# A planned linear-attention and expert kernel: 500 further plans, moved priorities, new transfer costs

## The chip, the cores and the metric

The kernel runs on one core of a Trainium2 chip. The time is the device time of one execution in microseconds, and lower is better. The kernel before took 289.69 us, the median of five runs.

A core has a matrix engine (TensorE, PE in the profile, with PEld for its weight loads), a vector engine (VectorE, DVE), a scalar engine (ScalarE, ACT), a general engine (GpSimd, POOL), and a sync engine (SP) that here only issues transfers. Each works through its own instructions in order; semaphores join them. TensorE writes its results to PSUM, a small memory of eight banks; ScalarE or VectorE read them from there ("evict" them).

## What is computed

```python
def _attn_ref(q, k, v, f_logit):                 # (4, 8, 768, 48) each
    f = 1.0 / (1.0 + np.exp(-f_logit))
    state = np.zeros((B, H, D, D))
    for t in range(S):
        state = f[:, :, t, :, None] * state + np.einsum('bhd,bhe->bhde', k[:, :, t], v[:, :, t])
        y[:, :, t] = np.einsum('bhd,bhde->bhe', q[:, :, t], state)
    return y

def _moe_ref(x, domain_probs, w1, w2):           # x (3072, 384), 4 experts, F = 1024
    p = domain_probs / (domain_probs.sum(-1, keepdims=True) + 1e-09)
    for e in range(E):
        h = np.maximum(x @ w1[e], 0.0)
        out += p[:, e:e + 1] * (h @ w2[e])
    return out
```

The attention's y, put side by side over the eight heads, is the experts' x. All four experts see all rows.

## The kernel before

The sequence of 768 is cut into six chunks `c` of 128 tokens, each with four batches `b`. For a chunk and batch the attention has these steps: `gate1` and `gate2` (ScalarE, the logarithm of the gate), `cs` (TensorE, a running sum by a triangular matrix), `exps` (ScalarE), the products `q` and `k` (VectorE or GpSimd), a transpose of them (`tpq`, `tpk` on TensorE for the first six pairs of chunk and batch, later a transposing DMA `tp` from the SP queue), `at` (TensorE, the scores), `ev_at0/1` (VectorE, with the mask), `y` (TensorE), its eviction `ev_y` or `ev_x0` to `ev_x3`, and a transpose `xt` (on TensorE with an eviction `ev_xt` for the first pairs, later a DMA). `kv`, `ev_kv` and `state` carry the state to the next chunk.

For the experts, `h c.e.fc.n0` is a unit of TensorE that computes block `fc` of expert `e`'s hidden layer for chunk `c`, from token column `n0` on (L410; three matmuls of 512 columns, or six of 128 in the first units of all), and `relu` of the same number evicts it on ScalarE (L421) or VectorE (L419). `o c.e.nt.half` is the second product for the first two chunks (L425, four matmuls). In the later chunks it is done in seven products `p1` to `p7` of sums (L473, the scheme of Strassen and Winograd), with the sums `s1` to `s4` of blocks of h (L459) before them and adds such as `c11+u1` (L479) behind them.

Weights come in 11 pieces issued by POOL (L267): pieces 0 and 1 are the halves of expert 0's w1, 2 and 3 those of expert 1's w1, 4 and 5 the halves of expert 0's w2 (the first half is needed by `o 0.0.*.0`, the second by `o 0.0.*.1`), 6 to 10 the rest whole. `ld` loads f, q, k and v over the SP queue (L258).

The order in which each engine works is not written by hand. Every step is recorded as an `Op` with a cost for each engine that could run it, a priority, the steps it depends on, the buffers that it takes and frees, and a `lag` (what passes from its end until another engine can use its result). `Plan.run` goes forward in modelled time: whenever an engine is free it takes, of the steps that are ready and for which a buffer is free, the one with the lowest priority number. `Plan.plan` does that twice; the second pass knows from the first when the transposing transfers will be wanted, and keeps big loads out of their way. The order that comes out is emitted. Nothing of the modelled times reaches the chip but the order, the engine chosen for each step, and the number of dummy matmuls (L865) with which TensorE is kept busy ahead of the first `h`.

The priorities say which work is urgent: loads and weights under -300, the first chunk's attention from -200 on, and after that units counted up from 0, with each chunk's attention laid between the units of the chunk before.

Of the kernel before, what the change touches and what calls it, by code (L numbers as in the profile page):

```python
# [1 line left out]

# [24 lines left out]
class Plan:  # L27
# [23 lines left out]
    def take(self, o):  # L51
        new = [k for k in o.takes if k not in self.slot]
        for r in {k[0] for k in new}:
            if len(self.rooms[r]) < sum(k[0] == r for k in new):
                return False
        for k in new:
            self.slot[k] = self.rooms[k[0]].pop(0)
        return True

    def plan(self, passes):  # L60
        rooms = {r: list(x) for r, x in self.rooms.items() if r != "ps_t"}
        for o in self.ops:
            if o.name.split(" ")[-1].startswith("0.") and set(o.costs) & {"ACT", "DVE"}:
                o.lag += 0.1
        soon = {}
        for i in range(passes):
            self.rooms, self.slot, self.left = {r: list(x) for r, x in rooms.items()}, {}, {}
            self.rooms["ps_t"] = self.rooms["ps_m"]
            for o in self.ops:
                o.end = o.start = o.engine = o.behind = None  # L70
            done = self.run(soon)
            soon = {o: self.ready(o, "DMA") for o in done if o.engine == "DMA" and o.name[:2] in ("tp", "xt")}
        return done

    def run(self, soon):
        for o in self.ops:
            for k in o.frees:
                self.left[k] = self.left.get(k, 0) + 1
        left = sorted(self.ops, key=lambda o: o.prio)
        free_at = {e: 0.0 for o in left for e in o.costs}  # L80
        free_at.update({"DMA": 0.8, "DVE": 5.0, "POOL": 3.5, "ACT": 2.1, "PE": 2.0})
        freeing, done, now = [], [], 0.0
        port, last = 0.0, None
        while left:
            for f in [f for f in freeing if f[0] <= now + 1e-9]:
                freeing.remove(f)
                self.rooms[f[1]].append(f[2])
            for e in ("PE", "ACT", "DVE", "POOL", "DMA"):
                while free_at[e] <= now + 1e-9:
                    for o in left:  # L90
                        if e == "DMA" and o.name.startswith("ld") and o.name[4:5] > "2" and any(
                                x.start is None and now < t < now + o.costs[e] - 0.3 for x, t in soon.items()):
                            continue
                        if e in o.costs and not (o.port and e in ("DVE", "POOL") and port > now + 1e-9):
                            t = self.ready(o, e)
                            if t is not None and t <= now + 1e-9 and self.take(o):
                                break
                    else:
                        break
                    left.remove(o)  # L100
                    if o.name == "h 0.0.0.0":
                        self.rooms["ps_m"].append(7)
                    o.engine, o.start, o.end = e, now, now + o.costs[e]
                    free_at[e] = o.end
                    if o.port and e in ("DVE", "POOL"):
                        if e == "POOL" and last is not None and last.engine == "DVE":
                            o.behind = last
                        port, last = o.end, o
                    for k in o.frees:
                        self.left[k] -= 1  # L110
                        if self.left[k] == 0:
                            held = o.lag if e == "DMA" or o.name.startswith("egs") else 0.0
                            freeing.append((o.end + held + self.LATENCY, k[0], self.slot[k]))
                    done.append(o)
            nexts = [t for t in free_at.values()] + [f[0] for f in freeing] + [port] + list(soon.values())
            for o in left:
                for e in o.costs:
                    nexts.append(self.ready(o, e) or 0.0)
            nexts = [t for t in nexts if t > now + 1e-9]
            if left and not nexts:  # L120
                raise RuntimeError("no step can run: " + ", ".join(o.name for o in left[:8]))
            if left:
                now = min(nexts)
        return done
# [3 lines left out]
def kernel(  # L128
# [12 lines left out]
    B, H, S, D = q.shape  # L141
# [344 lines left out]
    def add_load(c, nm, b, n, prio, deps=(), cost=None):  # L486
        op = P.add(f"ld {nm}{c}.{b}", {"DMA": cost or (1.05 if c else 1.1) * n}, lambda e: load(c, nm, b, n), prio,
                   deps=deps, takes=[(nm, c, b // 2)], lag=3.5 if c > 1 else 2.0)
        for i in range(n):
            ld[c, nm, b + i] = op  # L490
        return op
# [22 lines left out]
    for i, (e, which, ks, cols) in enumerate(pieces):  # L514
        if i == 7:
            add_load(1, "f", 0, 1, -454.5, deps=wd[2, 1], cost=0.1)
        if i == w_last:
            for x in ((1, "f", 1, 1), (1, "k", 0, 2), (1, "q", 0, 2), (1, "v", 0, 2)):
                add_load(*x, -430 + len(ld), deps=wd[3, 1])
        iss = P.add(f"w issue {i}", {"POOL": 0.8}, lambda _, i=i, x=(e, which, ks, cols): load_w(i, *x),  # L520
                    -600 + 3 * i, deps=issued[-1:] + ([ld[1, "k", 0]] if i == w_last else []))
        op = P.add(f"w {i}", {"DMA": 2.05 if i < 6 else 4.4}, lambda _: None, -400 if i == w_last else -460 + i, deps=[iss])
        issued.append(iss)
# [9 lines left out]
    def attention(c, slot, gran):  # L533
# [10 lines left out]
        for b in range(B):  # L544
# [27 lines left out]
            else:  # L572
                et = [P.add(f"tp {c}.{b}", {"DMA": 1.4}, on(dma_tp), s(4), deps=[qm, km, ydone.get((c - 1, B - 1))], takes=[("QK", c, b)],
                            frees=[("qk", c, b)], lag=2.5)]
# [10 lines left out]
        for b in range(B):  # L585
# [12 lines left out]
            if c >= S0:  # L598
                xdone[c, b] = {}
                xe = None  # L600
                for g in range(NG):
                    ex_ = []
                    for e in (2 * g, 2 * g + 1):
                        xe = P.add(f"ev_x{e} {c}.{b}", {"ACT": 0.58, "DVE": 0.63}, lambda eng, b=b, e=e: ev_x(c, b, e, eng), s(11) + 0.1 + 0.01 * e,
                                   deps=[y, pdone, xe], takes=[("yb", c, b, g)], frees=[pt_("y")])
                        ex_.append(xe)
                    xdone[c, b][g] = P.add(f"xt {c}.{b}.{g}", {"DMA": 1.2}, on(dma_xt, g), s(13) + 7 * g, deps=ex_, takes=[("xT", c, g)],
                                           frees=[("yb", c, b, g)], lag=2.4)
# [17 lines left out]
        for b in range(B if more else 0):  # L626
            on = lambda f, b=b: (lambda e: f(c, b))
            pt_ = lambda kind, b=b: ("ps_t", kind, c, b)
            s15 = slot(b, 15) if c else 2 + 2 * b
            kv = P.add(f"kv {c}.{b}", {"PE": 0.22}, on(pe_kv), s15, deps=[Y[b]] + (X[B - 1] if c == 0 else []),  # L630
                       takes=[pt_("KV")], frees=[("vb", c, b), ("qk", c, b)], lag=0.2)
# [22 lines left out]
    def add_o(c, e, nt, half):  # L654
# [9 lines left out]
        if half == 1 or by_cols:  # L664
# [5 lines left out]
            if e == E - 1:  # L670
                P.add(f"store {c}.{nt}.{part}", {"DMA": 0.73}, lambda _: store(c, nt, cols), p + (10 if c else 30), deps=[ev], frees=[room], lag=1.5)

# [21 lines left out]
    def add_p(c, g, r):  # L694
# [31 lines left out]
        def send(nm, i, j, us=slice(0, 2)):  # L726
            P.add(f"store {c}.{nm}.{us.start}", {"ACT": 0.6} if us.stop - us.start == 1 else {"DMA": 0.73}, lambda eg: store_c(c, i, j, o(nm), us, eg), p - 25, deps=[last.get((nm, us.start), last[nm])], frees=[("o", c, nm)], lag=1.5)

# [124 lines left out]

    done = P.plan(2)
    first = next(o for o in done if o.name.startswith("h 0.")).start
# [14 lines left out]

PRINT = None


# [28 lines left out]
```

## Time and profile before

| | |
|---|---|
| five runs | 289.88, 288.78, 288.94, 289.69, 289.84 us; median 289.69 |
| the profiled execution | 289.88 us, of which the span from the first to the last instruction is 288.1 |
| granted TensorE clock | mean 0.998; 1.00 from 3.85 us on |
| instructions | TensorE 2557 matmuls, VectorE 357, ScalarE 345, GpSimd 163 |
| transfers | 41.21 MB; the transposes of xT take 2.8 us from issue to landing in the median (5.7 at most), those of QK 3.3 (4.6 at most) |

The busy line over the span, in 40 slices of 7.2 us (a digit is the tenth of the slice in which the engine was busy):

```profile
PE   6988999999999999999999999999999999999994
DVE  4777234688576697396885788667785744942663
ACT  5766554847865677986787678687577664463430
POOL 3794300217488224725316585045080000000001
DMA  7999999995989999899969897987647130010003
```

In the timeline of the trace a row is a run of like instructions: start, length in us, engine, line, operation, what it writes and reads, how often, and in brackets the idle time before it with what ended it. The ends of matmuls are modelled and overlap, so starts are what to go by. In the list of waits the columns are the waiting engine and line, what it waited for, and the total, the number and the longest of the waits.

### The profile page before, as it was taken

The page shows a single profiled execution, that of the slowest core. Times are in us where ns is not written, and L with a number is a line of the kernel's source. Part 1 is how long each engine was busy: PE and PEld are TensorE (multiplying, and loading weights), DVE is VectorE, ACT ScalarE, POOL GpSimd, SP SyncE. Part 2 cuts the span into 40 slices and gives each one's busy share as a digit, 9 for nine tenths or more (in the row PEclk, how much of TensorE's full clock was granted, in tenths as well). Part 3 has the DMA queues.
Part 4 walks back from the last instruction along what each step waited for, and adds up shares of the span by engine and source line. Part 5 has one row for each costly group of instructions (what it writes and reads, how often), then busy time and mean ns, then how long its engine had stood idle before and what let it go on. Part 6 is the DMA issues. An engine that isn't in the chain of part 4 may idle for free.

```text
span 288.1 us, 6498 instructions
## 1 busy us (share of the span) xinstructions
PE 279.2 (97%) x2557; PEld 193.3 (67%) x2557; DVE 189.4 (66%) x357; ACT 183.3 (64%) x345; POOL 101.5 (35%) x163
## 2 busy tenths in 40 slices
PE   6988999999999999999999999999999999999994
PEld 2466555567777777458776767766767867678694
DVE  4777234688576697396885788667785744942663
ACT  5766554847865677986787678687577664463430
POOL 3794300217488224725316585045080000000001
PEclk9999999999999999999999999999999999999999
DMA  7999999995989999899969897987647130010003
GB/s 155 205 164 205 208 196 198 180 226 97 182 169 158 201 200 182 165 209 194 178 118 195 170 196 138 190 169 151 144 93 148 37 74 27 29 55 2 0 2 112
DMA packets 157331, 41.21 MB, mean 143 GB/s; under 512 B 145756, under 2 KB 156508, under 8 KB 157300
## 3 DMA queue, kind: packets, MB, share of 16 engines
q1 hardware_dynamic: 145764, 33.88, 61.0%
q0 software_dynamic: 11248, 6.72, 16.5%
q8 instruction: 20, 0.33, 0.5%
q10 hardware_dynamic: 288, 0.20, 0.2%
q14 instruction: 11, 0.09, 0.1%
HBM read 31.51 MB, written 4.72 MB: 126 GB/s over the span
## 4 chain that ended last, share of the span: by engine, by line
PE 89%; DMA 5%; SPq 2%; POOL 2%; issue 0%; DVE 0%
PE ps L410 41%; PE ps L473 26%; PE ps L425 15%; DMA w_sb<-in_moe_w_dram 4%; SPq L258 2%; PE ps L358 2%; DMA k<-in_k_dram 1%; PE ps L373 1%; PE ps L369 1%; PE ps L295 1%; POOL w_sb L267 1%; PE ps L379 1%; POOL vb L254 1%; PE ps L332 0%; DVE o L479 0%
## 5 line engine op out<-in xcount | busy, mean ns | idle before, releaser
L410 PE MATMUL ps<-xT,w_sb 128*128 128x512 bf16 (+3 forms) x720 | 144.0, 336 | 0.8 <-DMA w_sb<-in_moe_w_dram 0.5
L421 ACT ACTIVATE h<-ps 128x512 bf16<-128x512 f32 (+2 forms) x184 | 98.6, 543 | 62.1 <-PE ps L410 57.6
L410 PEld LDWEIGHTS <-w_sb 128*128 128x128 bf16 x720 | 65.9, 98 | 44.1 <-DMA w_sb<-in_moe_w_dram 0.6
L425 PE MATMUL ps<-w_sb,h 128*128 128x384 bf16 x256 | 50.4, 326 | 1.0 <-DMA w_sb<-in_moe_w_dram 1.0
L473 PEld LDWEIGHTS <-h 128*128 128x128 bf16 x512 | 42.8, 98 | 5.9
L479 DVE TENSOR_TENSOR o<-o,ps 128x384 f32<-128x384 f32 (+1 forms) x43 | 22.2, 532 | 25.3 <-PE ps L473 23.8
L362 DVE TENSOR_TENSOR AT<-ps,mask 128x512 bf16<-128x512 f32 x48 | 30.2, 683 | 10.0 <-PE ps L358 10.0
L425 PEld LDWEIGHTS <-h 128*128 128x128 bf16 x256 | 24.6, 98 | 16.7 <-DVE Sf L386 1.5
L473 PEld LDWEIGHTS <-s 128*128 128x128 bf16 x384 | 32.2, 98 | 4.4
L419 DVE TENSOR_SCALAR h<-ps 128x256 bf16<-128x256 f32 (+2 forms) x44 | 23.3, 541 | 14.7 <-PE ps L410 13.7
L315 ACT ACTIVATE e<-ps 128x384 f32<-128x384 f32 x48 | 26.7, 671 | 4.7 <-issue 2.2
L479 POOL TENSOR_TENSOR o<-o,o 128x384 f32<-128x384 f32 x5 | 5.0, 999 | 65.5 <-DVE o L479 65.5
L323 POOL TENSOR_TENSOR qk<-q,e 128x384 bf16<-128x384 f32 x18 | 21.5, 1197 | 17.1 <-ACT h L421 6.8
L390 POOL TENSOR_TENSOR Sf<-Sf,egs 112x192 f32<-112x192 f32 x20 | 10.4, 518 | 46.5 <-DVE Sf L386 10.9
L323 POOL TENSOR_TENSOR qk<-k,e 128x384 bf16<-128x384 f32 x20 | 20.3, 1014 | 16.7 <-ACT e L315 10.0
L342 ACT ACTIVATE yb<-ps,pn 128x384 bf16<-128x384 f32 x41 | 22.3, 587 | 4.1 <-PE ps L373 3.2
L473 PE MATMUL ps<-tw,h 128*128 128x192 bf16 x256 | 23.9, 246 | 0.0
L473 PE MATMUL ps<-w_sb,s 128*128 128x192 bf16 x256 | 23.9, 246 | 0.0
L473 PE MATMUL ps<-w_sb,h 128*128 128x192 bf16 x256 | 23.6, 246 | 0.0
L459 DVE TENSOR_TENSOR s<-h 128x1024 bf16<-128x1024 bf16 x16 | 11.2, 698 | 8.4 <-ACT h L421 8.0
L344 DVE TENSOR_SCALAR yb<-ps,pn 128x384 bf16<-128x384 f32 x23 | 13.8, 613 | 2.8 <-PE ps L373 1.9
L393 POOL CAST sb<-Sf 48x192 bf16<-48x192 f32 x40 | 14.5, 362 | 2.3
(74 smaller groups left out, 285.4 us busy)
## 6 DMA issues: line engine op xcount, KB each, us to landing
w_sb<-in_moe_w_dram POOLq DMA_DIRECT2D x5, 768.0 KB, 18.5
k<-in_k_dram SPq DMA_DIRECT2D x10, 384.0 KB, 5.5
q<-in_q_dram SPq DMA_DIRECT2D x10, 384.0 KB, 5.8
v<-in_v_dram SPq DMA_DIRECT2D x10, 384.0 KB, 4.8
out_dram<-o SPq DMA_DIRECT2D x19, 192.0 KB, 2.2
f<-in_f_logit_dram SPq DMA_DIRECT2D x9, 384.0 KB, 5.1
w_sb<-in_moe_w_dram POOLq DMA_DIRECT2D x6, 384.0 KB, 8.5
f<-in_f_logit_dram SPq DMA_DIRECT2D x6, 192.0 KB, 3.9
```

Of the source, the lines that this page charges most:

```text
L315: nc.scalar.activation(out=o, in_=i, func=AF.Exp, scale=1.0 if j else -1.0)
L323: return engines[eng].tensor_tensor(out=tl("qk", c, b)[:, j, :, 0:D].rearrange("t (i r) d -> t i r d", r=2), in0=tl("qk"[j], c, b // 2)[:, ...
L342: nc.scalar.activation(out=out, in_=in_, func=AF.Copy, scale=pe)
L344: nc.vector.tensor_single_scalar(out=out, in_=in_, scalar=pe, op=ALU.mult)
L362: nc.vector.tensor_tensor(out=tl("AT", c, b)[:, r], in0=tl("A", c, b, r), in1=mask01.unsqueeze(1).broadcast_to([T, NP, T]), op=ALU.mult)
L393: nc.gpsimd.tensor_copy(out=Sb[rows, b, :, r * D:(r + 1) * D], in_=Sf[rows, b])
L410: nc.tensor.matmul(out=hp(c, e, fc, n0, n1, nf)[:, f], lhsT=w1_sb[:, e, kk, (fc + f) * 128:(fc + f + 1) * 128], rhs=x_of(c, e)[:, kk, n0:n ...
L419: nc.vector.tensor_relu(out=dst, in_=src)
L421: nc.scalar.activation(out=dst, in_=src, func=AF.Relu)
L425: nc.tensor.matmul(out=tl("op", c, e, nt, part)[:, cols], lhsT=tl("h", c, e, half_of(c, nt * T))[:, fc, nt * T:(nt + 1) * T], rhs=w2_sb[:, ...
L473: nc.tensor.matmul(out=tl("pp_", c, g, bank(c, g, r, u))[:, u], lhsT=a[:, fc, u * T:(u + 1) * T], rhs=w[:, fc], start=(n + fc == 0 and (c, ...
L479: return engines[eng].tensor_tensor(out=o[:, us], in0=x[:, us], in1=y[:, us], op=ALU.add)
```

## The change

Three things change, and all of them act when the kernel is built.

First, the planner makes more plans. After the two passes of before it runs 500 rounds. Each picks a gap in TensorE's modelled work (longer gaps more often), picks one to three steps that ran from 15 us before it to 1 us after it, moves their priorities by up to 12 either way, and makes a new plan. The plan is kept where its score is lower. The score comes from `replay`, which holds the order fixed and computes the times again for three sets of costs (as given; transfers 3% longer; ScalarE, VectorE and GpSimd 5% longer), as the mean of TensorE's last end and the last end of all. Steps with priorities under -300 (loads of the first two chunks and weights) keep their priorities.

Second, some costs are other numbers: a load 1.0 for 1.05 per batch, the first weight piece 1.7 for 2.05, a lag of 0.6 for the other pieces, the transposes `tp` 1.45 for 1.4 and `xt` 1.1 for 1.2, stores 0.65 for 0.73, and `kv` on TensorE 0.17 for 0.22.

Third, `run` is rewritten so that 500 plans take less time to make: it holds the ready steps in sorted lists and no longer goes through all of them. It also keeps, for each buffer, which steps must have freed it (`o.after`), for the replay.

The core of the diff:

```diff
+    def replay(self, done, scale):
+        ends, free_at, port = {}, {}, 0.0
+        for o in done:
+            e = o.engine
+            t = max(free_at.get(e, 0.0), o.start if o.prio < -300 else 0.0)
+            for d in o.deps:
+                t = max(t, ends[d] + (d.lag * scale.get(d.engine, 1.0) + self.LATENCY if d.engine != e else 0.0 if e == "PE" else 0.05))
+            for d in o.after:
+                t = max(t, ends[d] + self.held(d) + self.LATENCY)
...
+            ends[o] = free_at[e] = t + o.costs[e] * scale.get(e, 1.0)
...
+    def score(self, done):
+        total = 0.0
+        for scale in SCENES:
+            ends = self.replay(done, scale)
+            total += 0.5 * (max(ends.values()) + max(t for o, t in ends.items() if o.engine == "PE"))
+        return total / len(SCENES)
+
+    def gaps(self, done):
+        out, t = [], 0.0
+        for o in done:
+            if o.engine == "PE":
+                if o.start > 19.5 and o.start - t > 0.08:
+                    out.append((o.start, o.start - t))
+                t = o.end
+        return out
+
-    def plan(self, passes):
+    def plan(self, rounds):
...
+        soon = wish(self.once({}))
+        done = self.once(soon)
+        best, rng = self.score(done), Random(3)
+        starts, gaps, ahead = {o: o.start for o in done}, self.gaps(done), wish(done)
+        for i in range(rounds):
+            t = rng.choices(gaps, [g[1] for g in gaps])[0][0]
+            near = [o for o in self.ops if t - 15.0 < starts[o] < t + 1.0 and o.prio > -300]
+            moved = [(o, o.prio) for o in rng.sample(near, min(len(near), rng.choice((1, 1, 2, 3))))]
+            for o, p in moved:
+                o.prio = p + rng.choice((-12, -6, -3, -1, 1, 3, 6, 12)) * rng.uniform(0.5, 1.0)
+            try:
+                done = self.once(ahead)
+                new = self.score(done)
+            except RuntimeError:
+                new = best
+            if new < best - 1e-6:
+                best, soon = new, ahead
+                starts, gaps, ahead = {o: o.start for o in done}, self.gaps(done), wish(done)
...
+            else:
+                for o, p in moved:
+                    o.prio = p
+        return self.once(soon)
...
-        op = P.add(f"ld {nm}{c}.{b}", {"DMA": cost or (1.05 if c else 1.1) * n}, lambda e: load(c, nm, b, n), prio,
+        op = P.add(f"ld {nm}{c}.{b}", {"DMA": cost or (1.0 if c else 1.1) * n}, lambda e: load(c, nm, b, n), prio,
...
-        op = P.add(f"w {i}", {"DMA": 2.05 if i < 6 else 4.4}, lambda _: None, -400 if i == w_last else -460 + i, deps=[iss])
+        op = P.add(f"w {i}", {"DMA": 1.7 if i == 0 else 2.05 if i < 6 else 4.4}, lambda _: None, -400 if i == w_last else -460 + i, deps=[iss], lag=0.6 if i else 0.0)
...
-            kv = P.add(f"kv {c}.{b}", {"PE": 0.22}, on(pe_kv), s15, deps=[Y[b]] + (X[B - 1] if c == 0 else []),
+            kv = P.add(f"kv {c}.{b}", {"PE": 0.17}, on(pe_kv), s15, deps=[Y[b]] + (X[B - 1] if c == 0 else []),
...
-    done = P.plan(2)
+    done = P.plan(ROUNDS)
...
+ROUNDS = 500
+SCENES = ({}, {"DMA": 1.03}, {"ACT": 1.05, "DVE": 1.05, "POOL": 1.05})
```

What that makes of TensorE's order up to the second products, by the steps' names (before on the left; steps in the same place on both sides between the blocks are left out):

```
y 0.1                              y 0.1
at 0.3, xt 0.1, y 0.2              h 0.0.0.0, y 0.2, at 0.3, xt 0.1
h 0.0.0.0, h 0.0.2.0               h 0.0.2.0, xt 0.2
h 0.0.0.128, h 0.0.2.128           h 0.0.0.128, h 0.0.2.128
xt 0.2, y 0.3                      h 0.0.0.256, y 0.3
h 0.0.0.256, h 0.0.2.256           h 0.0.2.256
h 0.0.4.0, xt 0.3 (2), h 0.0.5.0   h 0.0.4.0, h 0.0.5.0, xt 0.3 (2)
...
h 0.1.0.0, h 0.1.1.0               h 0.1.0.0, h 0.1.1.0, h 0.1.2.0
o 0.0.0.0, h 0.1.2.0               o 0.0.0.0
o 0.0.1.0, o 0.0.0.1               o 0.0.1.0, h 0.1.3.0, o 0.0.0.1
```

Ahead of that stretch the order is the same; three dummy matmuls stand before `at 0.3` in the one, two before `h 0.0.0.0` in the other. Further on the order differs in many places by a few steps, and 101 steps go to another engine, nearly all of them evictions between ScalarE and VectorE.

## The prediction

> **What bounds the kernel now.** I read four views in this order: the busy totals, TensorE's list of waits, the busy time by stretch, and TensorE's timeline around the only long waits. The totals first:
>
> ```profile
> span 288.1 us, 6498 instructions
> PE 279.2 (97%) x2557; PEld 193.3 (67%) x2557; DVE 189.4 (66%) x357; ACT 183.3 (64%) x345; POOL 101.5 (35%) x163
> ```
>
> No other engine is above 66%, so TensorE's own sequence sets the end, and a new order can win only where TensorE waits. All its waits are these (total, times, longest):
>
> ```profile
> PE ps L295 <- ACT gp L291: 1.7, 3, 0.8
> PE ps L865 <- DVE busy L171: 1.1, 1, 1.1
> PE ps L425 <- DMA w_sb<-in_moe_w_dram: 1.0, 1, 1.0
> PE ps L410 <- DMA w_sb<-in_moe_w_dram: 0.5, 1, 0.5
> PE ps L410 <- ACT xT L248: 0.4, 1, 0.4
> PE ps L332 <- ACT QK L248: 0.2, 1, 0.2
> ```
>
> They sum to 4.9 us, and the stretches say where they lie (the first number after the length is TensorE's busy time):
>
> ```profile
> 20.00:30.00 10.00, 8.59 (x106) 6.28 (x104) 6.17 (x19) 5.60 (x12) 5.70 (x12) 1.00 1.26 206
> 30.00:40.00 10.00, 10.00 (x56) 5.30 (x55) 3.53 (x6) 7.09 (x12) 1.68 (x3) 1.00 1.20 206
> ```
>
> From 30 us to 280 us every stretch has TensorE busy for its full 10.00. Since ends of matmuls are modelled, I checked this by starts: a 512-column matmul follows the one before it after 216 ns in the median, and the 456 of them lose 1.7 us over that in all, 1.2 of it in the wait at 28.84. So the middle of the kernel holds no wait to remove. What is open lies before 30 us:
>
> ```profile
> 17.21 0.81 PE L865 MATMUL ps<-busy 128*128 128x512 bf16 x3
> 17.95 0.40 PE L358 MATMUL ps<-QK 48*128 48x128 bf16 x8
> 18.28 0.34 PE L398 MATMUL ps<-ident,yb 128*128 128x128 bf16 x3
> 18.46 0.36 PE L373 MATMUL ps<-vb,AT 128*128 128x48 bf16 x8
> 19.29 1.51 PE L410 MATMUL ps<-xT,w_sb 128*128 128x128 bf16 x24 [0.47 <-DMA w_sb<-in_moe_w_dram]
> 20.64 0.33 PE L398 MATMUL ps<-ident,yb 128*128 128x128 bf16 x3
> 20.81 0.36 PE L373 MATMUL ps<-vb,AT 128*128 128x48 bf16 x8
> 21.54 1.32 PE L410 MATMUL ps<-xT,w_sb 128*128 128x128 bf16 x15 [0.37 <-ACT xT L248]
> ...
> 25.00 2.80 PE L410 MATMUL ps<-xT,w_sb 128*128 128x128 bf16 x30
> 28.84 0.81 PE L425 MATMUL ps<-w_sb,h 128*128 128x384 bf16 x4 [1.04 <-DMA w_sb<-in_moe_w_dram]
> 29.49 0.81 PE L410 MATMUL ps<-xT,w_sb 128*128 128x512 bf16 x3
> 30.14 1.46 PE L425 MATMUL ps<-w_sb,h 128*128 128x384 bf16 x8
> ```
>
> The chain that ended last passes through the same place: the transfer of weight piece 4 (first half of expert 0's w2), issued at 17.30, lands at 28.71, and from there to the end only matmuls follow.
>
> ```profile
> 17.30 11.41 DMA w_sb<-in_moe_w_dram
> 28.71 0.14 issue
> 28.84 0.81 PE ps L425 x4
> ```
>
> So: end = landing of piece 4, plus the TensorE work that stands behind it.
>
> **The change part by part.** *The planner and its costs* run when the kernel is built. Their edits put no instruction on the chip; all they do is the new order. The program loses one dummy matmul with its weight load (31 to 30) and otherwise keeps every operation. The SP queue is the same for its first 32 issues and the POOL queue for its first 23 steps, which hold all the weight issues. So the landings of pieces 0 to 4 stay: 19.24 for piece 0 (user at 19.29) and 28.71 for piece 4. This goes in as 0.
>
> *The gain, at piece 4.* In the new order the unit `h 0.1.2.0` (three 512-column matmuls, 29.49 to 30.14, so 0.65 us) stands ahead of `o 0.0.0.0`, the user of piece 4, and no longer behind it. It needs piece 2, there since 23.7. If TensorE reaches `o 0.0.0.0` before 28.84 even with this unit, the work behind piece 4 is shorter by 0.65.
>
> *Does it reach it?* Before: 25.00 plus 24 matmuls of 128 columns at 56 ns (19.29 to 20.64 holds 24) plus two units of 0.65 is 27.64: TensorE is ready then, and really waits 1.2. From 19.29 to 27.64 are 8.35 us, of which the wait for xT takes 0.52 (20.81 + 0.21 to 21.54). That leaves 7.83 of work. Now the loss: the new order has `h 0.0.0.0` (user of piece 0) ahead of `at 0.3`, `xt 0.1` and `y 0.2`, which ran before 19.29 under the wait for piece 0. They come behind it now: 0.33 (17.95 to 18.28) + 0.18 + 0.21 (17.00 to 17.21, the same eight matmuls) = 0.72. And a wait is new: `h 0.0.0.128` needs ScalarE's copy of `xt 0.1`. That transpose now ends at 19.29 + 0.34 + 0.72 + 0.16 (the modelled tail) = 20.51, the copy takes 0.48, the semaphore 0.05: 21.04. TensorE is through with `h 0.0.2.0` and `xt 0.2` at 20.86, so it waits 0.2; one relu stands between that copy and the next, which may add 0.1. Sum: 19.29 + 7.83 + 0.72 + 0.2 = 28.04, plus the moved unit 28.69, with the 0.1 28.79. Both are before 28.84, by 0.15 to 0.05. So the gain is the full 0.65, with little to spare: any later delay in this stretch takes it back one for one. If piece 4 were there early and nothing hid the delay, TensorE would end the unit at 28.69 and not at 27.64 + 0.65 = 28.29: a loss of 0.4. I take 0.65; the ends are +0.65 and -0.4.
>
> *The units behind.* `o 0.0.0.1` needs piece 5 and starts two units after `o 0.0.0.0` has ended, as before (30.79, landing 30.43). Piece 7 gets one unit more ahead of its user, so 0.65 later against a stream that is 0.65 earlier. Both at 0.
>
> *About 100 evictions change between ScalarE and VectorE*, none is added: 0 while TensorE's waits stay covered. The fullest 10-us stretches hold 8.91 (VectorE) and 8.70 (ScalarE). The tightest feeds behind 31 us in the timeline end 0.4 before their product starts (relu `3.3.7.0` before `p2 3.1.0` at 194.5, s2 before p6 at 277.5). Without that cover the eviction's delay is TensorE's: a relu (0.60 on ScalarE, 0.69 on VectorE) run one place later costs 0.2 to 0.3. The bound is +0.3 at a place or two.
>
> *Adds on GpSimd.* Three `c+u` adds go from VectorE (0.55) to GpSimd (1.00), one comes back, one cast goes to ScalarE. Behind them on POOL stand casts and products whose users are matmuls over 5 us later: 0; without that cover 0.45 each.
>
> *Moved transfers.* Ten-odd SP issues from the 33rd on change places, loads of chunks 4 and 5 among them. SP's transposes take 1.2 to issue and 2.8 (xT) or 3.3 (QK) to land in the median, 5.7 and 4.6 at most. The users nearest to them before are `h 2.0.0.0` (1.2 after the landing), `at 3.3` (1.4) and `at 3.1` (1.4). In the new order these users stand 3, 3 and 2 TensorE steps earlier and their transposes at the same place of SP's queue; what feeds those is mostly earlier too. I take 0; the bounds are 0 and 5.7 - 2.8 - 1.2 = +1.7 at one place.
>
> *The end.* The last 64 TensorE steps, 44 of VectorE and 37 of ScalarE are the same, so the 4 us from the last matmul to the end stay: 0.
>
> [...] The granted clock is 1.00 from 3.85 us to the end, over TensorE's waits of up to 1.2. With `at 0.3` and the rest moved, TensorE has nothing from 17.64 to 19.29: 1.65, longer than any such gap here. [...]
>
> [...] The 216 ns per 512 columns from start to start say that the array is fed without a break, and the sum goes by them.
>
> **The sum.** The profiled execution took 289.88 with a span of 288.1; 0.65 less is 289.23. It was among the slower of the five: the median is 0.19 lower. So 289.05, a span near 287.4.
>
> **Rivals.** *TensorE comes late to piece 4* (the new waits are 0.4 to 1.0 and not 0.2, or piece 4 lands earlier): gain 0.45 to -0.4, so 289.2 to 290.1, near 289.5. For it: the margin of 0.05 to 0.15. Against it: each term is a measured row.
>
> *Transposes land late* (slower): one of the three users above waits. For it: the spread of landings, and that big loads now share the queue elsewhere. Against it: xT and QK keep their places in the queue at those users. It decides once a landing is 1.2 later than the median; at the largest seen it costs 1.7, so 289.05 + 1.7 = 290.75.
>
> *The clock drops* in the 1.65 gap. The first six dummies ran at 0.43 a piece and not 0.215, so such a stretch costs 1.3; less the margin, 290.2.
>
> *The change does nothing to the time*: only if piece 4 no longer binds, which is the first rival.
>
> **How the numbers follow.** Forecast 0.66, late to piece 4 0.12, late transposes 0.18, clock 0.04. A measurement can tell about 0.3% (0.87 us) from no change. The forecast's 0.65 is below that, with a spread between runs of 1.1: I give 0.28 of it to faster by over 0.3% and 0.38 to within. The first rival adds 0.11 to within and 0.01 to slower, late transposes 0.03 and 0.15, the clock 0.04 to slower: faster 0.28, same 0.52, slower 0.20. The forecast's own range is 288.3 to 289.6 (the runs' spread round 289.05). Upwards the range goes on to 290.5, short of the full late transpose.
>
> **What would show it.** Right: TensorE's wait before L425's first matmul (`o 0.0.0.0`) shrinks from 1.04 to 0 to 0.2, that matmul still starts at 28.8, the wait for piece 0 grows to about 1.6, a new wait of 0.2 on ScalarE's xT copy appears near 20.9, and no wait comes after 31 us. Wrong: that matmul starts after 29.3, TensorE waits on xT or QK transposes after 90 us, or the granted clock falls below 1.00 near 19 us.

## The result and the profile after

The changed kernel took 290.78 us in the median of 33 runs (288.57 to 293.19), against 289.69 for the kernel before (59 runs, 288.65 to 291.49) on the same chip. The ratio is 1.0033, 95% interval 1.0019 to 1.0047: about 1 us slower. The two slowest of the 33 (293.03 and 293.19) count as slow runs and are not in the ratio. Its profiled execution took 290.98 with a span of 289.2, 1.1 more than the span of before. The totals and TensorE's waits (total, times, longest), from the page and the list of waits of after:

```profile
span 289.2 us, 6494 instructions
PE 280.1 (97%) x2556; PEld 193.8 (67%) x2556; DVE 191.2 (66%) x358; ACT 181.1 (63%) x343; POOL 104.7 (36%) x164
```

```profile
PE ps L492 <- DMA w_sb<-in_moe_w_dram: 1.6, 1, 1.6
PE ps L947 <- DVE busy L253: 1.1, 1, 1.1
PE ps L492 <- ACT h L503: 0.9, 1, 0.9
PE ps L377 <- ACT gp L373: 0.9, 1, 0.9
PE ps L492 <- DMA xT<-yb: 0.6, 1, 0.6
PE ps L414 <- ACT QK L330: 0.2, 1, 0.2
```

Lines are shifted by the diff: L492 was L410 (steps `h`), L507 was L425 (steps `o` of the first kind), L503 was L421 (relu on ScalarE), L424 and L429 were L342 and L347 (evictions into yb, transposes `xt`), L522 was L440 (stores), L340 was L258 (loads). In the altered kernels of the experiments lines lie up to 10 further on (L419 for L410, L501 for L492). The wait for piece 4 is gone, the wait for piece 0 is 1.6, and two waits are new: 0.9 for a relu and 0.6 for an `xt` transpose. TensorE's timeline of after at weight piece 4:

```profile
26.76 2.11 PE L492 MATMUL ps<-xT,w_sb 128*128 128x512 bf16 x9
28.71 1.46 PE L507 MATMUL ps<-w_sb,h 128*128 128x384 bf16 x8
```

`o 0.0.0.0` starts at 28.71 and waits for nothing, behind three units where two stood. At 37.14 TensorE starts `h 0.2.0.0`, 0.78 earlier than before (37.92). Of that, 0.65 is the moved unit, and 0.13 is `o 0.0.0.0` starting earlier (28.71 against 28.84). So far the change does what was forecast. TensorE's timeline around 112 us, after first, then before:

```profile
111.55 0.32 PE L377 MATMUL ps<-gp,Ub 128*128 128x384 bf16 x1
112.74 0.82 PE L492 MATMUL ps<-xT,w_sb 128*128 128x256 bf16 x6 [0.86 <-ACT h L503]
113.39 1.46 PE L507 MATMUL ps<-w_sb,h 128*128 128x384 bf16 x8
115.47 1.46 PE L492 MATMUL ps<-xT,w_sb 128*128 128x512 bf16 x6 [0.61 <-DMA xT<-yb]
116.76 0.81 PE L507 MATMUL ps<-w_sb,h 128*128 128x384 bf16 x4
```

```profile
113.02 2.11 PE L425 MATMUL ps<-w_sb,h 128*128 128x384 bf16 x12
114.97 0.33 PE L295 MATMUL ps<-gp,Ub 128*128 128x384 bf16 x1
115.13 0.81 PE L425 MATMUL ps<-w_sb,h 128*128 128x384 bf16 x4
115.78 1.89 PE L410 MATMUL ps<-xT,w_sb 128*128 128x512 bf16 x8
```

The first 512-column product is `h 2.0.0.0`. Before, four `o` steps of four matmuls and `cs 3.1` ran ahead of it (x12, x1, x4) and it waited for nothing. After, two `o` steps run ahead of it (x8), then TensorE waits, and `o 1.3.2.1`, `cs 3.1` and `o 1.3.3.1` come behind it: 0.65 + 0.16 + 0.65 = 1.46 us. `h 2.0.0.0` starts 0.31 earlier (115.47 against 115.78) and has 1.46 more behind it: 1.15 later at the end, which is the 1.1 of the spans. By starts the two new waits cost 1.02 and 0.78, which less the 0.78 won early is 1.0 as well.

Why the transposes were late is told by SP's queue; after first, then before (start, length of the issue):

```profile
103.37 1.24 SPq L429 DMA_TRANSPOSE xT<-yb  x1
104.66 0.57 SPq L522 DMA_DIRECT2D out_dram<-xT  x1
105.29 0.42 SPq L522 DMA_DIRECT2D out_dram<-o  x1
105.77 0.45 SPq L340 DMA_DIRECT2D q<-in_q_dram  x1
106.97 3.16 SPq L429 DMA_TRANSPOSE xT<-yb  x2
...
110.86 2.93 SPq L429 DMA_TRANSPOSE xT<-yb  x2
```

```profile
102.11 1.17 SPq L440 DMA_DIRECT2D out_dram<-xT  x1
103.37 1.25 SPq L347 DMA_TRANSPOSE xT<-yb  x1
104.67 0.58 SPq L258 DMA_DIRECT2D q<-in_q_dram  x1
105.44 3.14 SPq L347 DMA_TRANSPOSE xT<-yb  x2
108.63 1.04 SPq L440 DMA_DIRECT2D out_dram<-o  x2
109.78 4.25 SPq L347 DMA_TRANSPOSE xT<-yb  x3
```

`out_dram<-xT` is `store 0.3.0`; its result lies in a buffer that `xt 2.0.1` writes next. Behind `xt 2.1.0` in place of ahead of it, it is issued at 104.66 and not 102.11; in the trace it lands at 106.88, and `xt 2.0.1`, which needs its buffer, is issued at 106.97 and not at 105.44. `xt 2.2.0` follows at 110.86, 1.08 later than before. The chain of waits of after has the rest:

```profile
108.91 2.89 DMA xT<-yb
111.81 0.02 issue
111.83 0.08 ACT yb L424
111.91 0.40 issue
112.31 0.25 ACT h L503
112.56 2.78 DMA xT<-yb
115.33 0.14 issue
115.47 1.46 PE ps L492 x6
```

`xt 2.1.1` lands at 111.81 and frees its yb buffer; ScalarE, idle for 2.11 by its own timeline, can only then evict into it, the relu queued behind that (112.31) frees a PSUM bank for TensorE at 112.74, and `xt 2.3.0`, issued at 112.56, lands at 115.33. The queue's order is not the whole of it, though: in the profiles of e3 and e9 below, which have after's order of SP's queue, `xt 2.2.0` was issued at 109.36 and 109.01, earlier than in before (109.78).

The granted clocks of the timed runs tell one thing more. Of 34 runs of after (the profiled one among them), 11 have a mean granted clock of 0.995 or less; their median is 291.84, that of the other 23 is 290.42.

### The profile page after: what moved, and what is told of

Same layout as the page of the kernel before. It is cut to its first block, busy times and chain, and to the rows that moved or that the text cites. A ratio compares the mean times of both kernels' runs of the same rounds, so it can differ in the third digit from the quotient of the medians.

```text
span 289.2 us, 6494 instructions
## 1 busy us (share of the span) xinstructions
PE 280.1 (97%) x2556; PEld 193.8 (67%) x2556; DVE 191.2 (66%) x358; ACT 181.1 (63%) x343; POOL 104.7 (36%) x164
## 4 chain that ended last, share of the span: by engine, by line
PE 89%; DMA 5%; SPq 2%; issue 1%; POOL 1%; DVE 1%; ACT 0%
PE ps L492 43%; PE ps L555 26%; PE ps L507 13%; SPq L340 2%; DMA w_sb<-in_moe_w_dram 2%; PE ps L440 2%; DMA xT<-yb 2%; PE ps L455 1%; DMA k<-in_k_dram 1%; PE ps L451 1%; PE ps L461 1%; PE ps L377 1%; POOL vb L336 1%; DVE Sf L468 0%; PE ps L414 0%
## 5 line engine op out<-in xcount | busy, mean ns | idle before, releaser
L492 PE MATMUL ps<-xT,w_sb 128*128 128x512 bf16 (+3 forms) x720 | 143.2, 336 | 3.2 <-DMA w_sb<-in_moe_w_dram 1.6
L503 ACT ACTIVATE h<-ps 128x512 bf16<-128x512 f32 (+2 forms) x177 | 95.4, 546 | 67.8 <-PE ps L492 64.5
L492 PEld LDWEIGHTS <-w_sb 128*128 128x128 bf16 x720 | 65.6, 98 | 48.3 <-issue 2.2
L507 PE MATMUL ps<-w_sb,h 128*128 128x384 bf16 x256 | 49.8, 326 | 0.0
L507 PEld LDWEIGHTS <-h 128*128 128x128 bf16 x256 | 24.6, 98 | 15.5
L501 DVE TENSOR_SCALAR h<-ps 128x256 bf16<-128x256 f32 (+2 forms) x51 | 26.7, 540 | 10.7 <-PE ps L492 9.8
L561 POOL TENSOR_TENSOR o<-o,o 128x384 f32<-128x384 f32 x7 | 7.0, 997 | 63.5 <-DVE o L561 60.0
L424 ACT ACTIVATE yb<-ps,pn 128x384 bf16<-128x384 f32 x43 | 23.2, 582 | 5.4 <-PE ps L455 2.9
L468 DVE TENSOR_TENSOR Sf<-Sf,ps 48x192 f32<-48x192 f32 x40 | 14.0, 349 | 4.6 <-PE ps L461 3.9
L541 DVE TENSOR_TENSOR s<-h 128x1024 bf16<-128x1024 bf16 x16 | 12.6, 793 | 6.5 <-ACT h L503 6.1
L475 POOL CAST sb<-Sf 48x192 bf16<-48x192 f32 x40 | 15.4, 385 | 2.3
```

Of the source, the lines that this page charges most:

```text
L424: nc.scalar.activation(out=out, in_=in_, func=AF.Copy, scale=pe)
L468: nc.vector.tensor_tensor(out=Sf[rows, b], in0=Sf[rows, b], in1=KV[rows, :, r, :], op=ALU.add)
L475: nc.gpsimd.tensor_copy(out=Sb[rows, b, :, r * D:(r + 1) * D], in_=Sf[rows, b])
L492: nc.tensor.matmul(out=hp(c, e, fc, n0, n1, nf)[:, f], lhsT=w1_sb[:, e, kk, (fc + f) * 128:(fc + f + 1) * 128], rhs=x_of(c, e)[:, kk, n0:n ...
L501: nc.vector.tensor_relu(out=dst, in_=src)
L503: nc.scalar.activation(out=dst, in_=src, func=AF.Relu)
```

## The experiments

All ran beside runs of the kernel before on the same chip; its median was 289.65 us beside e1 to e4, 290.56 beside e5 to e8, 289.32 beside e9 to e12 and 289.63 beside e13 to e16, so ratios are what to compare across these groups. An order was altered in the finished plan by `moved(done, [(step, other)])`, which takes the step out and puts it directly ahead of the other; the diffs show that line. "Dropped" counts the runs whose mean granted clock was 0.995 or less.

### What each half of the change does

The changed kernel with the new costs and no search, and with the search and the old costs:

```diff
-ROUNDS = 500
+ROUNDS = 0
```

> The changed kernel with no search rounds: the new costs alone, two passes as before. Its order has the same first part as the changed kernel (h 0.0.0.0 ahead of at 0.3, h 0.1.2.0 ahead of o 0.0.0.0), so the gain of 0.65 and the clock gap are both there. Behind it xt 2.1.0 is ahead of store 0.3.0 in SP's queue too, and xt 2.3.0 stands two places later than in the changed kernel, behind xt 2.2.1 and a load, while its user h 2.0.0.0 stands two steps earlier on TensorE than before. If the costs are what made the transposes late, a wait of 2 us or more shows at h 2.0.0.0 and the time is 291 or above. If the search made them late, this kernel has no such wait and takes about 289.5.

Measured: 292.95, ratio 1.0085 (1.0055 to 1.0115), 6 of 12 dropped. In its profile TensorE waits 2.55 at `h 2.0.0.0` by starts (2.4 in the list of waits); `xt 2.3.0`, which stands behind a load there, is issued at 113.38, against 111.48 in before's trace.

```diff
-{"DMA": 1.7 if i == 0 else 2.05 if i < 6 else 4.4}, ..., lag=0.6 if i else 0.0)
+{"DMA": 2.05 if i < 6 else 4.4}, ...)
...
-{"DMA": 1.1}, on(dma_xt, g)
+{"DMA": 1.2}, on(dma_xt, g)
...
```

> The changed kernel with the costs of before: 500 rounds of search alone. Its order keeps at 0.3 and three dummies ahead of h 0.0.0.0 and keeps o 0.0.0.0 ahead of h 0.1.2.0, so there is neither the gain nor the gap: no low clocks, the wait for piece 4 stays at about 1.0. h 2.0.0.0 stands as before behind o 1.3.2.1 and o 1.3.3.1. If the costs alone make the loss, it takes what the kernel before takes, 289.7 within 0.2%. If a search over modelled times uses up slack wherever it is, waits of 0.5 to 1 us for transposes appear after 60 us, and the median is 290.2 or more.

Measured: 290.37, ratio 0.9997 (0.9974 to 1.0021), 1 of 12 dropped. So the new costs without the search lose clearly, and their plan already has the new front (`h 0.0.0.0` ahead of `at 0.3`). With the search, after's ratio is 1.0033: part of the loss is gone. The search alone moved nothing that can be measured. Which of the costs makes the loss was not run one by one.

### The early gain alone

```diff
     done = P.plan(2)
+    done = moved(done, [("h 0.1.2.0", "o 0.0.0.0")])
```

> The kernel before, with one step moved: the unit h 0.1.2.0 stands ahead of o 0.0.0.0 on TensorE, nothing else. If the early gain is real and by itself worth what the sum said, the wait for weight piece 4 shrinks from 1.04 to about 0.4 us, everything behind it comes 0.65 us earlier, the span goes from 288.1 to about 287.4, and the time is 0.2% below the kernel before. If the gain is given back somewhere later whatever the order behind it is, a wait of about 0.6 us turns up after 31 us and the time is the same as before.

```diff
+    done = moved(done, [("h 0.1.2.0", "o 0.0.0.0"), ("h 0.1.3.0", "o 0.0.0.0")])
```

> The kernel before with two units, h 0.1.2.0 and h 0.1.3.0, ahead of o 0.0.0.0. TensorE is ready at 27.64 us and two units take 1.30, so o 0.0.0.0 starts at about 28.94, 0.1 after it could. The whole wait of 1.2 us (by starts) is filled: span about 286.9 to 287.0, time 0.35 to 0.4% below before. If what stands behind has too little slack for 1.2 us, a transfer or an eviction becomes late and shows as a new TensorE wait after 31 us; the tightest transfer then was 1.2 us ahead of its user.

> The kernel of e2 once more, on this chip: before with h 0.1.2.0 and h 0.1.3.0 ahead of o 0.0.0.0. If the early gain is real and only partly absorbed at h 2.0.0.0: 0.2 to 0.9 us shorter than before, as in e2 (ratio 0.997). If it is absorbed there in most executions: 0 to 0.2 shorter. No dropped clock.

Measured: one unit 289.29, ratio 0.9984 (0.9964 to 1.0004). Two units 289.21, ratio 0.9970 (0.9947 to 0.9994); on another chip 289.11, ratio 0.9981 (0.9966 to 0.9997). None dropped. Two units ahead of the wait are worth about half a microsecond, and this small edit of the order beats both kernels. In e1's profile a wait of 0.8 by starts stood at `h 2.0.0.0`, where the profile of before had none: the gain made early can be lost there.

### The front and the clock

Six more dummies in after, which fill the gap ahead of piece 0:

```diff
+            o.pad += 6 * (o.name == "h 0.0.0.0")
```

> The changed kernel with six more dummy matmuls ahead of h 0.0.0.0 (1.3 us), which fill the 1.6 us in which TensorE has nothing to do before weight piece 0 lands. If that gap lets the clock drop in some executions (in a third of the changed kernel's timed runs the mean granted clock was 0.991 to 0.995, and those took about 291.5, the others about 290.4), no run of this kernel shows a clock under 0.997, and the median falls by about 0.4 us to 290.4. If the low clocks have another cause, about a third of the runs keep them and the median stays at 290.8. The two waits at 112.7 and 115.5 us stay in either case.

Measured: 289.96, ratio 1.0009 (0.9985 to 1.0033), 0 of 12 dropped. And before with after's front alone:

```diff
+    done = moved(done, [("h 0.0.0.0", "at 0.3")])
...
+            o.pad = 2 if o.name == "h 0.0.0.0" else o.pad
```

> The kernel before with one step moved, h 0.0.0.0 ahead of at 0.3, and with two dummies in front of it, as in the changed order: TensorE has nothing to do for about 1.6 us before weight piece 0 lands, and all else is the order of before. Piece 4 still binds (TensorE is ready near 28.1 of 28.8), so by the order alone the time is the same as before. Theory of the clock: about a third of the runs show a mean clock of 0.995 or less and take some 1.5 us more; the median goes up by 0.2 to 0.5. Rival, that the low clocks of the changed kernel have another cause: at most one run in twelve, as before (1 of 35).

Measured: 291.87, ratio 1.0031 (1.0000 to 1.0061), 4 of 12 dropped (292.46 to 293.91), the other eight 291.13 in the mean. The front alone brings the drops, the dummies take them away. That the eight undropped runs lie 0.6 above the mean of before beside them (290.55) is not explained by the clock. Over all kernels, 30 of 94 runs with this front and without the dummies dropped, 1 of 134 runs of before beside these experiments, and 2 of 126 of the other altered kernels (0 of the 48 with the six dummies). The profile of the next kernel (SP's order, below) caught one. Its busy time by stretches (after the engines' busy times: the granted clock, the DMA share and GB/s) and its wait:

```profile
14.00:19.86 5.86, 3.92 (x50) 2.29 (x47) 4.10 (x8) 2.66 (x4) 5.10 (x7) 1.00 1.52 157
19.86:26.69 6.83, 6.31 (x68) 5.79 (x69) 2.99 (x6) 2.70 (x7) 2.59 (x3) 0.50 1.27 204
26.69:31.00 4.31, 4.31 (x57) 3.38 (x56) 3.31 (x12) 2.86 (x7) 1.01 (x3) 1.00 1.20 212
```

```profile
PE ps L501 <- DMA w_sb<-in_moe_w_dram: 2.2, 1, 2.2
```

TensorE waits 2.2 us for piece 0, and within that wait the clock goes to 0.50 and stays there for 6.83 us. The same wait was 1.6 in after's profile, 2.2 in e7's and 2.8 in e6's, and there the clock held (means of 0.998, 1.000 and 0.998): with a wait of 2.2 it dropped in e4's execution and not in e7's. This execution has the lowest mean clock of the 30 (0.988); the others have 0.991 to 0.995. Half the clock lost for 6.83 of its 291.3 us is this execution's 0.988; by the same sum, 0.994 is a stretch of about 3.5 us at 0.50, an estimate.

### SP's order

```diff
+    done = moved(done, [("store 0.3.0", "xt 2.1.0"), ("store 1.0.0", "store 1.1.0")])
```

> The changed kernel with two stores put back where the kernel before had them in SP's queue: store 0.3.0 ahead of the transpose xt 2.1.0, store 1.0.0 behind xt 2.1.1. Theory of the queue: xt 2.0.1 waits in the queue until store 0.3.0 has landed and freed its xT buffer (106.88); with the store 1.2 us earlier, xt 2.0.1 and xt 2.1.1 issue and land some 1.3 us earlier, the eviction ev_x2 2.3 no longer blocks ScalarE, the 1.0 us wait for PSUM at 112.7 goes, and xt 2.3.0 lands near 114.0, so that h 2.0.0.0 waits about 0.4: span 287.8, time 1.3 us under the changed kernel. Rival, that the evictions moved between ScalarE and VectorE make the waits: both waits stay, 1.0 and 0.8, and the time is the changed kernel's.

Measured: 290.63, ratio 1.0022 (0.9992 to 1.0052), 3 of 12 dropped. The wait for the relu is gone from its profile, and 0.24 is left at `h 2.0.0.0`; the time hardly follows. Its profile is the one with the dropped clock, and the profile of e3, with after's order of SP's queue, has neither wait, so the missing waits don't speak for the queue's order. Next the two units of e2 in before, together with two stores moved behind the transposes:

```diff
+    done = moved(done, [("h 0.1.2.0", "o 0.0.0.0"), ("h 0.1.3.0", "o 0.0.0.0"), ("store 1.0.0", "xt 2.2.1"), ("store 1.1.0", "xt 2.2.1")])
```

> Before with h 0.1.2.0 and h 0.1.3.0 ahead of o 0.0.0.0, as in e2, and with store 1.0.0 and store 1.1.0 behind xt 2.3.0 in SP's queue instead of ahead of xt 2.2.0 (1.04 us of issues). Theory 1: xt 2.2.0 and xt 2.3.0 are issued and land up to 1.0 earlier, h 2.0.0.0 waits less: 0.3 to 1.0 less than the two units alone (which took 0.44 off), 0.7 to 1.4 less than before. Theory 3 (the transposes wait for their yb buffers and evictions and not for the queue): as e2, 0.4 less than before, xt 2.2.0 issued at the same time.

Measured: 289.63, ratio 1.0004 (0.9986 to 1.0022), none dropped. That is no better than the two units without it (0.9970 and 0.9981). Neither shows a gain from SP's order. Their intervals leave room for some tenths of a microsecond, and in e7 a transpose that stood later in the queue came with a wait of 2.55.

### What stands behind the transposes

The two `o` steps put back ahead of `h 2.0.0.0` in after:

```diff
     done = P.plan(ROUNDS)
+    done = moved(done, [("o 1.3.2.1", "h 2.0.0.0"), ("o 1.3.3.1", "h 2.0.0.0")])
```

> Theory 1 (what stands behind the transposes costs): in the profiles so far the end lies 172.3 to 172.5 us behind the start of h 2.0.0.0 in the order of before and 173.7 to 173.75 in that of after, the difference being o 1.3.2.1, cs 3.1 and o 1.3.3.1 (0.65 + 0.16 + 0.65). With the two o steps ahead of h 2.0.0.0 again and nothing else changed from after, 1.30 us of work lies over the wait: 0.6 less than after where the wait was 0.6 as in its profile, up to 1.3 less where it is longer; the end should lie 172.4 to 172.6 behind the start of h 2.0.0.0. Theory 2 (the clock alone made after slower): as after, within 0.3 us. On both, about a third of the runs still have a mean granted clock of 0.995 or less, since the front is after's.

Measured: 289.78, ratio 1.0022 (0.9994 to 1.0050), 3 of 12 dropped. Then the reverse, in before, one step of TensorE moved, by three places and by five:

```diff
     done = P.plan(2)
+    done = moved(done, [("h 2.0.0.0", "o 1.3.2.1")])
```

> Before with one step of TensorE moved: h 2.0.0.0 stands ahead of o 1.3.2.1, so that 1.46 us of work stand behind the transposes, as in after. Theory 1: 0.3 us longer than before in an execution like its profile (slack 1.2), 1.46 longer where h 2.0.0.0 waits in the order of before too (0.8 to 1.1 in the profiles of three kernels with that order), so 0.3 to 1.5 longer in the median; the end 173.7 to 173.8 behind the start of h 2.0.0.0. Theory 2 (a step's place among its neighbours costs nothing there): 0, within 0.3. No run with a dropped clock, since the front is before's.

```diff
+    done = moved(done, [("h 2.0.0.0", "o 1.3.2.0")])
```

> Before with h 2.0.0.0 moved ahead of o 1.3.2.0: o 1.3.2.0, o 1.3.3.0, o 1.3.2.1, cs 3.1 and o 1.3.3.1, 4 x 0.65 + 0.16 = 2.76 us, stand behind the transposes that h 2.0.0.0 reads. Theory 1 (what stands behind the transposes costs): the end 175.0 to 175.2 us behind the start of h 2.0.0.0; 1.6 us longer than before where xt 2.3.0 lands as in before's profile (114.58), 2.76 longer where it lands later than TensorE's own arrival; in the median 1.3 to 2.8 longer. Theory 2 (the place of the step costs nothing): 0, within 0.4. No dropped clock.

Measured: 289.98, ratio 1.0021 (0.9995 to 1.0048), with 1.46 us behind; 291.63 in six runs, ratio 1.0078 (1.0048 to 1.0108), with 2.76 behind. One of e13's six dropped, none of e10's. In the list of waits, e13's wait carries no name; the instructions on the tile xT between 105 and 120 us name it (who waited for the transposes, and from issue to landing):

```profile
  PE ps L419: 2.4, 1
...
DMA to landing us min/median/max: 2.8/3.1/5.4
```

TensorE waits 2.4 for the transposes, and all 2.76 us of the moved steps follow. What then stands behind `h 2.0.0.0` shows in the spans, without a comparison of times:

| order at `h 2.0.0.0` | profiled executions | span less start of `h 2.0.0.0` |
| --- | --- | --- |
| as before | before, e1, e5, e6, e8, e9, e12, e14, e16 | 172.2 to 172.5 |
| as before | e11; e2 (0.7 of it a wait for a QK transpose at 131.9 us) | 172.7; 173.1 |
| 0.81 us moved behind it | e7 | 173.0 |
| 1.46 us moved behind it | after, e15, e3, e4, e10 | 173.7 to 173.8 |
| 2.76 us moved behind it | e13 | 175.0 |

The start itself went from 114.3 (e9) to 118.5 (e6) in kernels with the order of before at this place. The span is that start plus one of these sums. Work moved behind `h 2.0.0.0` costs what it adds to TensorE's wait there: by starts that wait is 2.57 of the 2.76 in e13, but only 0.30 of the 1.46 in e10 (0.78 in after, 0.33 in e15, 0.24 in e4, none in e3). By this reckoning it is paid in full in an execution where TensorE had waited there already; where the transposes have slack, only what exceeds the slack. e10's single runs, six from 288.9 to 289.6 and six from 290.3 to 292.6, would fit that, but its interval does not exclude 1.

With the order of before at this place TensorE waited in five of eleven profiles: 0.8 in e1 and e8, 1.0 in e6, 1.1 in e5, 0.25 in e16. The rows of e6:

```profile
116.87 0.81 PE L434 MATMUL ps<-w_sb,h 128*128 128x384 bf16 x4
118.53 1.67 PE L419 MATMUL ps<-xT,w_sb 128*128 128x512 bf16 x7 [0.85 <-PE ps L434]
```

The bracket names TensorE itself, but in all five traces the matmul starts 0.09 to 0.13 after `xt 2.3.0` has landed. What differs is that transpose's time from issue to landing: 4.0 to 4.6 us in these five, 2.8 to 3.1 in before, e2, e9 and e14, which did not wait (in e11 and e12 the trace has no landing for it).

### After once more, and repaired

> After, unchanged, beside the others on this chip. 0.5 to 1.5 us longer than before; 3 to 5 of 12 runs with a mean granted clock of 0.995 or less; in its profile the end 173.7 to 173.8 us behind the start of h 2.0.0.0.

Measured: 290.63, ratio 1.0048 (1.0024 to 1.0072), 3 of 12 dropped; 288.6 - 114.85 = 173.75 in its profile.

```diff
+    done = moved(done, [("o 1.3.2.1", "h 2.0.0.0"), ("o 1.3.3.1", "h 2.0.0.0")])
...
+            o.pad += 6 * (o.name == "h 0.0.0.0")
```

> After with six more dummies ahead of h 0.0.0.0 and with o 1.3.2.1 and o 1.3.3.1 ahead of h 2.0.0.0; SP's queue as in after. Theory 1 (clock and work behind the transposes are the whole loss): no dropped clock; 0.7 to 1.6 us shorter than after on this chip, and 0 to 0.6 shorter than before (the early gain, as far as the later transposes leave it). Theory 4 (the rest of the new order costs too): no dropped clock, but 0.2 to 0.8 longer than before.

Measured: 289.85, ratio 1.0008 (0.9992 to 1.0024), none dropped: 0.8 shorter than e15 beside it, and not shorter than before. With SP's order repaired too, first the two stores of e4, then the stores of e11 as well:

```diff
+    done = moved(done, [("store 0.3.0", "xt 2.1.0"), ("store 1.0.0", "store 1.1.0"), ("o 1.3.2.1", "h 2.0.0.0"), ("o 1.3.3.1", "h 2.0.0.0")])
...
+            o.pad += 6 * (o.name == "h 0.0.0.0")
```

> The changed kernel with three things put right together: the six dummies of e3, the two stores of e4, and o 1.3.2.1 and o 1.3.3.1 back ahead of h 2.0.0.0 on TensorE. If the clock gap and the late transposes at 112 to 116 us are all that the changed order lost, only the gain at weight piece 4 is left: no run with a clock under 0.997, no wait over 0.3 us between 100 and 120 us in the profile, median about 289.1, 0.2% under the kernel before. If waits of the same kind come up at other places too, the median stays at 289.6 or more, and the profile names the place.

```diff
+    done = moved(done, [("store 0.3.0", "xt 2.1.0"), ("store 1.0.0", "xt 2.2.1"), ("store 1.1.0", "xt 2.2.1"), ("o 1.3.2.1", "h 2.0.0.0"), ("o 1.3.3.1", "h 2.0.0.0")])
```

> After with six more dummies ahead of h 0.0.0.0, store 0.3.0 ahead of xt 2.1.0, the stores 1.0.0 and 1.1.0 behind xt 2.3.0, and the two o steps ahead of h 2.0.0.0: all that was found, at once. Theory 1: no dropped clock, 1.0 to 2.0 less than after, and 0.2 to 1.2 less than before. Theory 3: as e5, equal to before.

Measured: 290.57, ratio 0.9999 (0.9976 to 1.0022), and 289.73, ratio 1.0012 (0.9996 to 1.0029); none dropped in either. So every kernel with the dummies is back at the time of before (0.9999 to 1.0012), and that holds for e3 as well, where nothing else was put right. That the two `o` steps give more on top is not shown (1.0008 with them in e16, 1.0009 without them in e3), and SP's order adds nothing that shows. For the steps speaks a comparison of the runs that did not drop: their median is 290.42 for after in e15, against 289.63 for before beside it, and 289.30 for e9, against 289.32. What stays open: e16 still has the early gain, worth 0.5 in e14 on the same chip, and yet is no faster than before. Its profile has, by starts, a wait of 0.8 near 61 us for a weight piece, and one of 0.9 near 14 us for a product on VectorE, but one execution can't say which wait is typical.

## Why the prediction was wrong

**The bound and the gain at piece 4: right.** The forecast had TensorE at `o 0.0.0.0` without a wait at 28.8 and a wait of 1.6 for piece 0; measured are 28.71 and 1.6. The extra wait of 0.2 for ScalarE's copy did not come. The stream was 0.78 ahead at 37 us, the forecast 0.65.

**"So the middle of the kernel holds no wait to remove": this step failed first.** It was read from one execution, in which `xt 2.3.0` had landed 1.2 before its user. The same order at this place waited for 0.8 (e1) and 1.0 (e6), because the transpose landed 4.0 to 4.5 after its issue and not 3.1. The 0.65 was added to the end as if nothing behind piece 4 could bind; in some executions the transposes do, at `h 2.0.0.0`, and take part of it or all.

**"Moved transfers ... I take 0": the term that was mis-sized.** The text named `h 2.0.0.0`, said that it stands three TensorE steps earlier, and gave its slack as 1.2. It did not take the 1.46 us of those three steps from that slack, which leaves -0.26, nor the 0.78 by which the stream comes earlier, nor charge the 1.46 that now stands behind a transfer. "What feeds those is mostly earlier too" did not hold in after's profile either: `xt 2.2.0` was issued 1.08 later, behind `store 0.3.0` (in e3 and e9, with the same queue, it was issued earlier than in before). The rival "transposes land late" named the place and, with 290.75, nearly the time. Its size came from the largest landing seen, though, and not from the moved work, and part of the measured loss is the clock's, so the near number is chance. e13 (+2.0, clear of noise) shows that work moved behind the transposes has a price; e10's 1.0021 points the same way but is not clear of noise. How the rest of the loss divides between this work, SP's order and the spread of the landings stays open.

**"The clock drops", 0.04: priced too low.** The prediction saw that the new gap of 1.65 was longer than any in the profile of before, and left it at that. No run shows how long a gap must be to drop the clock, so the 0.04 was the author's estimate; the runs showed about a third: 30 of 94 with this front dropped, in whose profiles the wait is 0.8 to 2.8 us, and the one drop that was profiled, 0.50 for 6.83 us, came in a wait of 2.2. Nor was the clock of before 1.00 "to the end": its trace has 0.50 from 287.15 us on, 2.9 us behind TensorE's last work (284.3). By after's own runs, a third of which are 1.4 longer (291.84 less 290.42), this is about 0.5 of the 1.0, an estimate; e3, with the dummies, stands 0.8 below after's median. The other two thirds, at 290.42, are still 0.7 above before, where the forecast had 0.65 below.

**Evictions, adds, pieces 5 and 7, the end: 0, not contradicted.** After's profile shows no wait of TensorE on VectorE or GpSimd but the one for the first dummies, which before has too. The one for a relu came from the late transpose: in e3 and e9, with the same queue, `xt 2.1.1` landed at 110.17 and 110.05 and not at 111.81, and that wait is absent.

## What to carry to other kernels

A slack read from one execution is a sample: before a step is moved ahead of a transfer, subtract from its slack everything that no longer runs ahead of it, and what the stream gains earlier. Work moved behind a transfer that binds is paid in full or nearly (a wait of 2.57 for 2.76 us of work in e13), and a gain made ahead of it may be lost there. A planner that counts a transfer at a nearly fixed cost (here as given or 3% longer) sees neither; a margin for late transfers in the score suggests itself, but was not tried here. Keep TensorE supplied with dummies where a first load decides: with the six dummies 0 of 48 runs here had a dropped clock, with this front and without them 30 of 94.

## What the runs showed of the hardware

In e4's profile the clock fell to 0.50 in a wait of 2.2 us and stayed there for 6.83 us, while in the profiles of e7 and e6 waits of 2.2 and 2.8 left the mean granted clock at 1.000 and 0.998. What decides between such executions is not shown: only one drop early in a kernel was profiled. In e13 an `xt` transpose held SP's queue for 1.2 us at the least and up to 3.6 (1209, 1247 and 3613 ns as minimum, median and maximum of seven) where the plans count 1.1 or 1.2, and landed 2.8 to 5.4 us after its issue.
